# A fused attention and two-layer gated MLP on one core: explicit periods for the weight conversions and x operands among the heads, tiles laid out by their time of death, and the last heads' normalization moved to the MLP's list

## Chip, core and metric

One NeuronCore of a Trainium2 chip runs the whole program as one launch. The time is the device time of one execution in microseconds (us), as the median of several; lower is better. The engines are TensorE (PE in the rows; its weight loads are PEld), VectorE (DVE), ScalarE (ACT), GpSimd (POOL) and SyncE (SP, which here only issues transfers; SPq and ACTq are the rows of queues).

## What is computed

Causal attention with a position bias over 4 batches of 8 heads, 576 positions, head size 64; its output, as 2304 tokens of 512 features, goes through two gated layers of width 1536, both with weights that arrive as 64-bit floats:

```python
cum = np.cumsum(np.maximum(s, 0.0), axis=-1)
bias = -(cum[:, :, :, None] - cum[:, :, None, :])
scores = np.where(causal, -1e9, q @ k.T / sqrt(64) + np.minimum(bias, 0.0))
attn = softmax(scores) @ v
x = attn.transpose(0, 2, 1, 3).reshape(2304, 512)
x = (sigmoid(x @ w_gate) * (x @ w_val)) @ w_out
out = ((x @ w_a) * (x @ w_b)) @ w_out2
```

## The kernel before, in words

**Two lists.** The program is two functions, `attention` and `mlps`, each of which fills a `Schedule` with operations (engine, duration, closure, dependencies, priority, a pool slot that it takes or gives back) and emits them. Every engine then runs its own instructions strictly in the emitted order, and waits at the first one whose inputs or buffers are not ready. `attention` is emitted with `in_order=True`: always the ready operation with the lowest priority number, where an operation whose pool has no free slot is passed over until one is given back. The priorities are places on a nominal time line in periods of HT = 6.1 us, one per head; head i begins at 6.1 i. `mlps` is emitted by the list's own simulation: each engine takes the lowest-numbered operation that is ready at the simulated time, with the durations and latencies (`lat`) that the operations carry.

**The heads.** Per head PE computes row maxima's scores (L550, L555), transposes the maxima (L570), computes the transposed scores (L587, L588) and the product with v (L624). ACT splits q and k (L520, L521), copies the transposed maxima out of PSUM (L572, "mc") and sends them on (L574), takes the exponentials (L593) and copies the product (L633, "xc"). The maxima's PSUM tile `ps_t` is used again by the last piece of the transposed scores, so PE's L587 on `ps_t` waits for ACT's L572. DVE takes maxima (L563) and low parts (L524, L526); POOL masks (L609) and normalizes (L637, "xm"). The normalization of a pair of heads is a chain through memory: L635 stores the sums, L651 and L652 invert them, L660 stores, L657 spreads them over the partitions ("rb"), L637 multiplies, L641 stores the pair into `x_sb` ("xd"). SP issues nearly all transfers, one queue for all of them, the small ones `o<-rel` (L530) and `o<-relq_d` (L531) of each head among them.

**Weights among the heads.** A matrix half (512 KB of 64-bit words) is loaded into one of three `raw` tiles (L194, "wl"), turned to 32 bits by one ACT instruction (L215) and four DVE instructions (L216 to L223), and gate and value halves are combined (`combine`): sums on DVE (L255, "ws"), high parts on ACT (L265, "wh"), low parts on POOL (L268, "wr"). The third piece of `wr` in order gives back the first `raw` tile of a pair, the last gives back the second. Six halves are converted among the heads (three column blocks of the first layer's weights), two of the three pairs are also combined there. Before, half e was placed at period 4e-2, with ACT's first step 2 periods later and `combine` spread over the 14 periods after the second half; with three `raw` tiles, halves 3, 4 and 5 find no free tile at their own priority.

**x operands.** The MLP multiplies by Strassen-like seven products, each in high and low parts (three matmuls, `passes`, L289 to L291). For each of three token blocks the operands are four sums (L317, "xs"), seven high parts on ACT (L320, "xh"), and seven low parts (L323, "xl"). Those of block 0 are made among the last heads (sums on POOL, low parts on DVE); the sums lie in two `stg` tiles.

**The MLP.** For each layer 12 column blocks c of the weights times 3 token blocks b give 36 units of 42 matmuls; a unit's results go through ACT (L780), DVE (L783, L794) and POOL (L796) to memory (`hd`, L798). The down product then reads them back (L859), splits them (L862 on ACT, L863 on DVE) and multiplies. Its input slots lie in one of the three operand regions (`H0`, `H1` in that of block 1), and the later half of its weights (L842, L843) in that of block 0; both need that block's last unit to be done (`last_of`).

**Memory.** `alone` opens one pool per tile. Attention's tiles grow from the right end of SBUF, the constants and the MLP's tiles from the left. A tile of the MLP that covers an address of attention waits for the last use of what lay there. Before, the order of declaration was not chosen: `wk2`, `rg1`, `rg2`, then `s0` to `s7` and `hs0` to `hs2` from the left; `rb`, `xt`, `xp`, `sc` at the right end, so that `s` and `hs` lie where `rb`, `xt` and `xp` lay.

Of the kernel before, what the change touches and what calls it, by code (L numbers as in the profile page):

```python
# [119 lines left out]
def attn_mlp_kernel(  # L120
# [14 lines left out]
    nc = tc.nc  # L135
# [112 lines left out]
    def combine(sc, n, done, prio, at):  # L248
# [22 lines left out]
        sc.op(("ws", n, 0), "DVE", 0.85, lambda: sums(0), list(done), prio + at[0], acq=("W", n))  # L271
        sc.op(("ws", n, 1), "DVE", 0.85, lambda: sums(1), [("ws", n, 0)], prio + at[1])
# [55 lines left out]

    def attention():
        with ExitStack() as c2:  # L330
# [6 lines left out]
            pdr = c2.enter_context(tc.tile_pool(name="at_dr", bufs=1, space=bass.MemoryType.DRAM))  # L337
# [7 lines left out]
            NO, NR2, NX = 4, 3, 5  # L345
            small = tile1([128, 1], FP32, "small")
            base = small[:, 0:1]
            rb_t = [tile1([128, S], FP32, f"rb{i}") for i in range(2)]
            xt = [tile1([128, S], FP32, f"xt{i}") for i in range(NX)]
            xp = [tile1([128, S], FP32, f"xp{i}") for i in range(2)]  # L350
            sc_t = [tile1([128, S // D], FP32, f"sc{i}") for i in range(2)]

            vx_t = [tile1([128, NC, 2 * D], FP32, f"vx{i}") for i in range(2)]

            P0 = [0, 576, 1024, 1344, 1536]
# [3 lines left out]
            mkb = tile1([128, 256], BF16, "mkb")  # L359
            mr_t = [tile1([NC, 128], F32R, f"mr{i}") for i in range(3)]  # L360
            nm_t = [tile1([128, 8], FP32, f"nm{i}") for i in range(4)]

            CQ1, CK1 = 0, 640
            o_t = [tile1([128, CK1 + S], F32R, f"o{i}") for i in range(NO)]
            p_t = [tile1([128, 2 * S], F32R, f"o2_{i}") for i in range(3)]
            r_t = [tile1([128, S], FP32, f"r{i}") for i in range(NR2)]
# [4 lines left out]
            rel = tile1([128, 2, S], F32R, "rel")  # L373
            sel, neg1 = pt_t[1][0:NR, S:2 * S], pt_t[2][0:3, S:2 * S]
            stg = [tile1([128, 2 * NP], FP32, f"stg{i}") for i in range(2)]
# [286 lines left out]

            for i in range(NH):
                head(i)

            for e in range(6):
                n, m = e // 2, e % 2
                prio = HT * (4 * e - 2) + WLATE * (e == 0)
                last = convert(sc, n, m, [("S", 4 * e - 3, 0)], prio,
                               at=[2 * HT + 1.2, 3 * HT - 0.15, 3 * HT - 0.14, 4 * HT - 0.15, 5 * HT - 0.15])  # L670
                if m == 1 and n < 2:
                    combine(sc, n, [prev_last, last], prio,
                            [6 * HT - 0.15, 10 * HT - 0.15] + [(7 + j) * HT + 0.2 if j == 0 or j == 3 else (10 + j) * HT + 0.2 for j in range(4)]
                            + [(11 + j) * HT + 3.2 for j in range(4)])
                prev_last = last
# [3 lines left out]
            done = [("xd", i) for i in range(H)]  # L679
            for k, (name, p, q, _) in enumerate(XS):  # L680
                op(("xs", name), "Pool", 2.1, x_sum(nc.gpsimd, get, 0, k), done + [("xs", z) for z in (p, q) if z[0] == "S"] + [("xs", "S3")] * (name == "S4"),
                   HT * (23 + k + (k > 1)) + 3.5, acq=("stg", name))
            for k, name in enumerate(["S3", "S1", "A11", "S2", "A12", "A22", "S4"]):
                op(("xh", name), "ACT", 0.75, x_high(rg, get, 0, name), done + [("xs", name)] * (name[0] == "S"), HT * (24 + k) + 1.7)
                op(("xl", name), "DVE", 0.96, x_low(nc.vector, rg, get, 0, name), [("xh", name)] + [("xs", z) for z in BEFORE[name]], HT * (25 + k) - 0.15,
# [4 lines left out]
    def mlps():  # L690
        def tile1(shape, dtype, name):
            return alone(ctx, shape, dtype, name)

        wslot.append(tile1([128, 2, WC], F32R, "wk2"))
# [280 lines left out]
```

## Time and profile before

| | us |
|---|---|
| median of 3 runs (lowest, highest) | 1125.54 (1125.07, 1128.4) |
| the profiled execution | 1125.24 |
| its span, first to last instruction | 1123.5 |
| PE busy in the span | 1049.9 (93%) |
| DVE, ACT, POOL busy | 723.9, 476.8, 384.2 |
| mean granted TensorE clock | 0.971 |

The heads fill about the first 254 us of the span, the first layer's units and down product the time to about 693 us, the second layer the rest. A row of a timeline has the start, the duration (of a merged row the length it covers), the engine, the line, the operation, what is written and read, and in square brackets how long the engine stood idle before it and what ended that. A row of waits has the total, the count and the longest. A row of windows has, per engine, busy time and the number of instructions begun, then the granted TensorE clock, where 1.00 is the 2.4 GHz level and 0.50 the 1.2 GHz level.

### The profile page before, as it was taken

The numbers are of one execution on the slowest core, as the hardware profiler recorded it, in microseconds if no ns is written. First come the engines' busy times: TensorE is split into PE (matmuls) and PEld (weight loads), VectorE is DVE, ScalarE is ACT, GpSimd is POOL, SyncE is SP. The second block draws the span as 40 slices with busy tenths as digits, with TensorE's granted clock in tenths as the row PEclk, the third lists the DMA queues.
The fourth block names the chain that finished last, engine by engine and source line by source line (L and its number), as shares of the span: only waits on it lengthen the run. The fifth ranks groups of instructions, "written<-read, shape, count | busy, mean of one in ns | idle before, by whom it ended". The sixth has DMA issues, their size and how long they took to land.

```text
span 1123.5 us, 16123 instructions
## 1 busy us (share of the span) xinstructions
PE 1049.9 (93%) x5638; PEld 955.7 (85%) x5638; DVE 723.9 (64%) x1137; ACT 476.8 (42%) x890; POOL 384.2 (34%) x363
## 2 busy tenths in 40 slices
PE   6999597894899999999899999899999999899998
PEld 4878486683899999999788889799999999788886
DVE  6786576765947876566983626966886676942222
ACT  3665364554445544455543325423443333422221
POOL 4135245556424452343320203525543333300000
PEclk9999898896999999999999999999999999899999
DMA  5466465443114433233664333214423224643342
GB/s 146 130 174 173 118 166 149 124 113 120 43 46 132 128 117 110 94 123 141 230 192 133 115 95 127 66 57 131 132 94 132 75 100 160 201 138 114 114 122 94
DMA packets 105871, 139.55 MB, mean 124 GB/s; under 512 B 32547, under 2 KB 67035, under 8 KB 105790
## 3 DMA queue, kind: packets, MB, share of 16 engines
q1 hardware_dynamic: 102542, 133.57, 38.2%
q10 hardware_dynamic: 2896, 4.81, 1.7%
q8 instruction: 44, 0.72, 0.2%
q14 instruction: 37, 0.30, 0.1%
q0 software_dynamic: 352, 0.16, 0.1%
HBM read 85.43 MB, written 33.33 MB: 106 GB/s over the span
## 4 chain that ended last, share of the span: by engine, by line
PE 78%; DVE 7%; DMA 5%; issue 4%; POOL 3%; ACT 1%; SPq 1%; ACTq 0%; POOLq 0%; DVEq 0%
PE ps L291 22%; PE ps L289 22%; PE ps L290 22%; PE ps_x L624 5%; PE ps_g L550 2%; POOL xp L637 1%; DVE hs L317 1%; PE ps_e L587 1%; PE ps_e L588 1%; PE ps_g L555 1%; DVE s L783 1%; POOL wk L268 1%; DVE nm L563 1%; DVE u L218 1%; DMA raw<-in_moe_w_val_dram 1%
## 5 line engine op out<-in xcount | busy, mean ns | idle before, releaser
L289 PE MATMUL ps<-rg,wk 128*128 128x384 f32 (+2 forms) x1128 | 385.3, 342 | 27.3 <-ACT s L780 19.3
L291 PE MATMUL ps<-rg,wk 128*128 128x384 f32 (+2 forms) x1128 | 383.7, 340 | 0.0
L289 PEld LDWEIGHTS ps<-rg,wk 128*128 128x128 f32 x1128 | 213.9, 190 | 35.3 <-ACT s L780 21.9
L291 PEld LDWEIGHTS ps<-rg,wk 128*128 128x128 f32 x1128 | 213.9, 190 | 3.8
L783 DVE TENSOR_TENSOR s<-ps,s 128x384 f32<-128x384 f32 x216 | 118.3, 553 | 125.6 <-PE ps L291 72.4
L290 PE MATMUL ps<-x_sb,wk 128*128 128x384 f32 x576 | 193.6, 336 | 0.0
L290 PE MATMUL ps<-rg,wk 128*128 128x384 f32 (+2 forms) x552 | 190.2, 345 | 2.1 <-DVE rg L863 2.1
L780 ACT COPY s<-ps 128x384 f32<-128x384 f32 x216 | 103.1, 480 | 185.5 <-PE ps L291 184.4
L796 POOL TENSOR_TENSOR hs<-s,s 128x384 f32<-128x384 f32 x72 | 80.4, 1116 | 264.5 <-issue 94.1
L268 POOL TENSOR_TENSOR wk<-raw,wk 128x512 fp32r<-128x512 f32 (+1 forms) x96 | 129.1, 1370 | 94.6 <-PE ps L291 54.8
L863 DVE TENSOR_TENSOR rg<-rg 128x512 fp32r<-128x512 f32 (+1 forms) x120 | 82.9, 699 | 116.3 <-ACT rg L862 114.3
L862 ACT CAST rg<-rg 128x512 fp32r<-128x512 f32 (+1 forms) x120 | 68.2, 577 | 159.3 <-DMA rg<-hd 128.6
L290 PEld LDWEIGHTS ps<-rg,wk 128*128 128x128 f32 x552 | 105.0, 190 | 6.2 <-DVE rg L863 2.4
L624 PE MATMUL ps_x<-pt,vx 128*128 128x256 f32 (+1 forms) x434 | 105.9, 387 | 4.2 <-ACT xt L633 2.9
L290 PEld LDWEIGHTS ps<-x_sb,wk 128*128 128x128 f32 x576 | 108.9, 189 | 0.3
L563 DVE TENSOR_REDUCE nm<-ps_g 128x1 f32<-128x512 f32 (+4 forms) x154 | 74.5, 534 | 41.2 <-PE ps_g L555 40.8
L624 PEld LDWEIGHTS ps_x<-pt,vx 128*128 128x128 f32 x434 | 80.1, 201 | 23.2 <-ACT xt L633 3.8
L609 POOL TENSOR_SCALAR_AFFINE_SELECT pt<-pt 128x256 f32<-128x256 f32 (+1 forms) x96 | 43.1, 468 | 132.9 <-ACT pt L593 132.0
L289 PE MATMUL ps<-rg,rg 128*128 128x512 f32 (+1 forms) x228 | 86.1, 378 | 0.0
L290 PE MATMUL ps<-rg,rg 128*128 128x512 f32 (+1 forms) x228 | 86.1, 378 | 0.0
L291 PE MATMUL ps<-rg,rg 128*128 128x512 f32 (+1 forms) x228 | 86.1, 378 | 0.0
L215 ACT ACTIVATE mag<-raw 128x512 f32<-128x512 f32 x72 | 48.5, 673 | 66.9 <-DVE raw L223 36.0
(110 smaller groups left out, 1549.8 us busy)
## 6 DMA issues: line engine op xcount, KB each, us to landing
hd<-hs SPq DMA_DIRECT2D x72, 384.0 KB
rg<-hd SPq DMA_DIRECT2D x72, 256.0 KB
raw<-in_moe_w_out_dram SPq DMA_DIRECT2D x24, 512.0 KB
r<-in_qk_dram SPq DMA_DIRECT2D x32, 288.0 KB
rg<-hd SPq DMA_DIRECT2D x72, 128.0 KB
raw<-in_moe_w_gate_dram SPq DMA_DIRECT2D x12, 512.0 KB
raw<-in_moe_w_val_dram SPq DMA_DIRECT2D x12, 512.0 KB
raw<-in_moe_w_a_dram SPq DMA_DIRECT2D x12, 512.0 KB
```

What stands on the lines that cost most here:

```text
L215: ("ACT", 0.6, lambda: nc.scalar.activation(out=mag, in_=parts(n, m)[1].bitcast(FP32), func=ACTF.Abs)),
L268: return lambda: nc.gpsimd.tensor_tensor(out=wcols(n, a, w, 1), in0=src(), in1=f32(wcols(n, a, w, 0)), op=ALU.subtract)
L289: nc.tensor.matmul(out=outp, lhsT=wh, rhs=xh, start=start and e == 0, stop=False, skip_group_check=True)
L290: nc.tensor.matmul(out=outp, lhsT=wh, rhs=xl, start=False, stop=False, skip_group_check=True)
L291: nc.tensor.matmul(out=outp, lhsT=wl, rhs=xh, start=False, stop=stop and e == n - 1, skip_group_check=True)
L563: nc.vector.tensor_reduce(out=nm[0:n, c:c + 1], in_=ps[0:n, p0:p0 + nk], axis=AX.X, op=ALU.max)
L624: nc.tensor.matmul(out=px[:, 256 + a:256 + q1_], lhsT=vx[:, j], rhs=pt[:, p0:p0 + q1_ - a], start=j == 0, stop=j == js[-1])
L780: op((x,) + key, "ACT", ACT_P, lambda x=x: nc.scalar.copy(out=s(x), in_=bank("X")), [P(p)], end(p) - 2, acq=("s", key + (x,)))
L783: return lambda: nc.vector.tensor_tensor(out=s(x), in0=bank(b_), in1=s(x), op=ALU.add)
L796: op(("h2",) + key, "Pool", PTT, lambda: nc.gpsimd.tensor_tensor(out=half(1), in0=s("s4"), in1=s("s2"), op=ALU.mult), [("c22",) + key, (g[ ...
L862: op(("hh",) + key, "ACT", 0.17 + 0.00083 * N, lambda hs=hs, N=N: nc.scalar.copy(out=hs()[:, 0, 0:N], in_=f32(hs()[:, 1, 0:N])), [("hl",) ...
L863: op(("ho",) + key, "DVE", 0.157 + 0.00104 * N, lambda hs=hs, N=N: nc.vector.tensor_tensor(out=hs()[:, 1, 0:N], in0=f32(hs()[:, 1, 0:N]), ...
```

## The change

The weight halves get explicit periods: a load, ACT's first step and DVE's steps for each of the six, and `combine` of the two pairs in 4 successive periods right after its sums. The x operands of block 0 get their own periods for sums, high parts and low parts. Attention's tiles are declared by their time of death: those of the last normalizations (`xt`, `rb`, `xp`, `sc`) in a stack of their own, `tails`, at the right end, then the others, the first to die on the inner side; on the MLP's side `s` and `hs` come first, then `rg1` and `wk2`, and `rg2` only when block 2 first asks for it, when `tails` is closed. Ten operations of the last four heads (the spread of pair 14, the whole chain of pair 15 after its sums, the four products, the two stores) are taken out of attention's list and put at the head of the MLP's. The simulation's latencies of weight sums, operand sums and high parts in the MLP rise from 0.2 to 1.0, 1.2 and 0.6 us. The last column block's units run in the order 1, 0, 2 of the token blocks instead of 0, 1, 2.

```diff
@@ convert / combine @@
-        sc.op(("ws", n, 0), "DVE", 0.85, lambda: sums(0), list(done), prio + at[0], acq=("W", n))
-        sc.op(("ws", n, 1), "DVE", 0.85, lambda: sums(1), [("ws", n, 0)], prio + at[1])
+        sc.op(("ws", n, 0), "DVE", 0.85, lambda: sums(0), list(done), prio + at[0], acq=("W", n), lat=1.0)
+        sc.op(("ws", n, 1), "DVE", 0.85, lambda: sums(1), [("ws", n, 0)], prio + at[1], lat=1.0)
@@ attention @@
+            def tile2(shape, dtype, name):
+                return alone(tails, shape, dtype, name, side="right")
...
+            xt = [tile2([128, S], FP32, f"xt{i}") for i in range(NX)]
+            rb_t = [tile2([128, S], FP32, f"rb{i}") for i in range(2)]
+            xp = [tile2([128, S], FP32, f"xp{i}") for i in range(2)]
+            sc_t = [tile2([128, S // D], FP32, f"sc{i}") for i in range(2)]
...
+            LATE = NH // 2 - 2
             for i in range(NH):
                 head(i)
-
-            for e in range(6):
+            for n in [("rb", LATE)] + [(k, j) for k in ("rc", "rd", "rb") for j in range(LATE + 1, NH // 2)] + \
+                    [("xm", i) for i in range(2 * LATE, NH)] + [("xd", j) for j in range(LATE, NH // 2)]:
+                late[n] = sc.ops.pop(n)
+
+            LOADS = [(-1, 1, 2), (2, 4, 5), (5, 8, 10), (12, 13, 14), (13, 16, 19), (20, 21, 22)]
+            SUMS = [(8, 9, 9), (17, 18, 17)]
+            for e, (ld, ab, dv) in enumerate(LOADS):
                 n, m = e // 2, e % 2
-                prio = HT * (4 * e - 2) + WLATE * (e == 0)
-                last = convert(sc, n, m, [("S", 4 * e - 3, 0)], prio,
-                               at=[2 * HT + 1.2, 3 * HT - 0.15, 3 * HT - 0.14, 4 * HT - 0.15, 5 * HT - 0.15])
+                prio = HT * ld + (0.5 if e > 2 else 0)
+                last = convert(sc, n, m, [("S", max(ld - 1, 0), 0)], prio,
+                               at=[HT * ab + 1.2 - prio] + [HT * (dv + k) - 0.15 + y - prio for k, y in ((0, 0), (0, 0.01), (1, 0), (2, 0))])
                 if m == 1 and n < 2:
-                    combine(sc, n, [prev_last, last], prio,
-                            [6 * HT - 0.15, 10 * HT - 0.15] + [(7 + j) * HT + 0.2 if j == 0 or j == 3 else (10 + j) * HT + 0.2 for j in range(4)]
-                            + [(11 + j) * HT + 3.2 for j in range(4)])
+                    s0, s1, h0 = SUMS[n]
+                    combine(sc, n, [prev_last, last], 0.0,
+                            [HT * s0 - 0.15, HT * s1 - 0.15] + [HT * (h0 + k) + 0.2 for k in (0, 2, 1, 3)] + [HT * (h0 + k) + 3.2 for k in (0, 2, 1, 3)])
...
+            AT_S = {"S1": 23, "S3": 24, "S2": 26, "S4": 28}
+            AT_H = {"A11": 24, "S3": 25, "S1": 26, "S2": 27, "A22": 28, "S4": 29, "A12": 30}
+            AT_L = {"S3": 26, "S1": 28, "A11": 29, "S2": 30, "A22": 30.2, "A12": 31, "S4": 31.2}
-                   HT * (23 + k + (k > 1)) + 3.5, acq=("stg", name))
-            for k, name in enumerate(["S3", "S1", "A11", "S2", "A12", "A22", "S4"]):
+                   HT * AT_S[name] + 3.5, acq=("stg", name))
...
@@ mlps @@
+        s_t = [tile1([128, NP], FP32, f"s{i}") for i in range(8)]
+        hs_t = [tile1([128, 2 * NP], FP32, f"hs{i}") for i in range(3)]
+        region.append(tile1([128, RC], F32R, "rg1"))
         wslot.append(tile1([128, 2, WC], F32R, "wk2"))
-        region.extend(tile1([128, RC], F32R, f"rg{i}") for i in (1, 2))
...
+            if k == len(region):
+                tails.close()
+                region.append(tile1([128, RC], F32R, f"rg{k}"))
...
-        op("tail", "Pool", 4.0, lambda: None, [], -1000)
+        op("tail", "ACT", 1.0, lambda: None, [], -1000)
+        op("sd", "SP", 0.5, lambda: None, ["tail"], -999, lat=2.5)
+        for k, (nm, (eng, dur, fn, deps, _, _, _, _)) in enumerate(late.items()):
+            op(nm, eng, dur, fn, deps + ["tail" if nm == ("rb", 14) else "sd"], -500 + k, lat={"rd": 3.5, "rb": 3.5, "xd": 3.0}.get(nm[0]))
...
-            return [(c, b) for b in range(NBK) for c in range(3)] + [(c, b) for c in range(3, KF) for b in range(NBK)]
+            return [(c, b) for b in range(NBK) for c in range(3)] + [(c, b) for c in range(3, KF - 1) for b in range(NBK)] + [(KF - 1, b) for b in (1, 0, 2)]
...
+            if L == 0 and b == 2:
+                deps = [k for k in late if k[0] == "xd"]
```

## Rows read from the trace of the kernel before

**Rows 1.** Waits of PE, 0 to 300 us: total us, times, longest
```profile
PE ps_t L587 <- ACT mr L572: 19.9, 4, 5.7
PE ps L289 <- ACT s L780: 15.7, 2, 13.9
```
**Rows 2.** Waits of PE, 296 us to the end (all of them)
```profile
PE ps L289 <- DVE s L783: 5.0, 2, 3.3
PE ps L289 <- ACT rg L862: 4.4, 2, 2.3
PE ps L289 <- ACT s L780: 3.6, 4, 1.3
PE ps L290 <- DVE rg L863: 2.1, 1, 2.1
PE ps L291 <- DVE rg L863: 1.3, 1, 1.3
```
**Rows 3.** Timeline of ACT, the first and last of four stops
```profile
116.46 0.68 ACT L215 ACTIVATE mag<-raw 128x512 f32<-128x512 f32 x1 [7.75 <-DMA raw<-in_moe_w_val_dram]
...
200.78 0.83 ACT L320 CAST rg<-stg 128x768 fp32r<-128x768 f32 x1 [6.31 <-POOL stg L317]
```
**Rows 4.** Timelines of POOL and SP, what those two stops waited behind
```profile
111.07 1.29 POOL L268 TENSOR_TENSOR wk<-raw,wk 128x512 fp32r<-128x512 f32 x1
...
112.80 0.40 SPq L194 DMA_DIRECT2D raw<-in_moe_w_val_dram  x1
...
198.44 2.31 POOL L317 TENSOR_TENSOR stg<-x_sb 128x768 f32<-128x768 f32 x1
```
**Rows 5.** Timeline of ACT, L572 of heads 14, 18, 22, 26 and 31
```profile
103.35 0.26 ACT L572 CAST mr<-ps_t 5x128 fp32r<-5x128 f32 x1 [0.61 <-PE ps_t L570]
...
144.94 0.26 ACT L572 CAST mr<-ps_t 5x128 fp32r<-5x128 f32 x1 [2.52 <-PE ps_t L570]
...
169.19 0.26 ACT L572 CAST mr<-ps_t 5x128 fp32r<-5x128 f32 x1 [0.49 <-PE ps_t L570]
...
209.48 0.26 ACT L572 CAST mr<-ps_t 5x128 fp32r<-5x128 f32 x1 [2.69 <-PE ps_t L570]
...
241.67 0.26 ACT L572 CAST mr<-ps_t 5x128 fp32r<-5x128 f32 x1 [1.94 <-PE ps_t L570]
```
**Rows 6.** Timelines of SP and PE, a weight load among undisturbed heads
```profile
58.52 0.60 SPq L194 DMA_DIRECT2D raw<-in_moe_w_gate_dram  x1
...
66.30 0.70 PE L550 MATMUL ps_g<-o 128*128 128x512 f32 x3 [1.05 <-DMA o<-relq_d]
```
**Rows 7.** Timelines of POOL, DVE, ACT and PE where the MLP begins
```profile
263.52 2.86 POOL L637 TENSOR_TENSOR xp<-xt,rb 64x576 f32<-64x576 f32 x2 [1.87 <-DMA rb<-rr_d]
...
272.81 5.05 POOL L323 TENSOR_TENSOR rg<-hs,rg 128x768 fp32r<-128x768 f32 x2
...
266.42 0.96 DVE L317 TENSOR_TENSOR hs<-x_sb 128x768 f32<-128x768 f32 x1 [8.96 <-POOL xp L637]
...
269.61 2.08 DVE L317 TENSOR_TENSOR hs<-x_sb 128x768 f32<-128x768 f32 x1
...
267.41 0.83 ACT L320 CAST rg<-hs 128x768 fp32r<-128x768 f32 x1 [10.54 <-DVE hs L317]
...
270.81 0.69 PE L289 MATMUL ps<-rg,wk 128*128 128x384 f32 x1 [13.85 <-ACT s L780]
...
276.64 0.34 PE L291 MATMUL ps<-rg,wk 128*128 128x384 f32 x1
...
278.75 0.34 PE L291 MATMUL ps<-rg,wk 128*128 128x384 f32 x1
```
**Rows 8.** Windows of 5 us where the two down products begin, and a steady one
```profile
540.00:545.00 5.00, 2.87 (x8) 2.20 (x8) 5.00 (x8) 4.03 (x8) 2.50 (x2) 0.78 1.01 387
...
555.00:560.00 5.00, 5.00 (x24) 4.14 (x23) 4.83 (x7) 2.84 (x5) 1.68 (x1) 1.00 0.68 221
...
965.00:970.00 5.00, 3.54 (x9) 2.73 (x10) 5.00 (x9) 3.21 (x7) 0.98 (x1) 0.60 0.94 321
```

More of the change, by code (lines that the diff above doesn't have):

```diff
@@ L326, in attn_mlp_kernel @@
     BEFORE = {"A11": ["S2", "S3"], "A12": ["S4"], "A22": ["S1"], "S1": ["S2"], "S2": ["S4"], "S3": [], "S4": []}
+    late = {}
+    tails = ExitStack()
     def attention():
@@ L335, in psum1 @@
                 return alone(c2, [128, n], FP32, name, space=PSUM)
[L337 removed]
+            def tile2(shape, dtype, name):
+                return alone(tails, shape, dtype, name, side="right")
+            pdr = tails.enter_context(tc.tile_pool(name="at_dr", bufs=1, space=bass.MemoryType.DRAM))
             SUP = 1.0 / scale
@@ L359, in attention @@
             mkb = tile1([128, 256], BF16, "mkb")
+            nm_t = [tile1([128, 8], FP32, f"nm{i}") for i in range(4)]
+            stg = [tile1([128, 2 * NP], FP32, f"stg{i}") for i in range(2)]
             mr_t = [tile1([NC, 128], F32R, f"mr{i}") for i in range(3)]
-            nm_t = [tile1([128, 8], FP32, f"nm{i}") for i in range(4)]
-            CQ1, CK1 = 0, 640
             o_t = [tile1([128, CK1 + S], F32R, f"o{i}") for i in range(NO)]
             p_t = [tile1([128, 2 * S], F32R, f"o2_{i}") for i in range(3)]
+            rel = tile1([128, 2, S], F32R, "rel")
             r_t = [tile1([128, S], FP32, f"r{i}") for i in range(NR2)]
@@ L372, in attention @@
             mkf, zer = pt_t[1][:, 0:128], pt_t[2][:, 0:S]
-            rel = tile1([128, 2, S], F32R, "rel")
             sel, neg1 = pt_t[1][0:NR, S:2 * S], pt_t[2][0:3, S:2 * S]
-            stg = [tile1([128, 2 * NP], FP32, f"stg{i}") for i in range(2)]
             def load_qk(i):
@@ L699, in rgn @@
         def rgn(L, b):
-            return region[(b + 2 * L) % NBK]
+            k = (b + 2 * L) % NBK
+            if k == len(region):
+                tails.close()
+                region.append(tile1([128, RC], F32R, f"rg{k}"))
+            return region[k]
         NH_ = RC // (2 * NB)
         sc = Schedule({
-            "s": [tile1([128, NP], FP32, f"s{i}") for i in range(8)],
-            "hst": [tile1([128, 2 * NP], FP32, f"hs{i}") for i in range(3)],
+            "s": list(s_t),
+            "hst": list(hs_t),
             "ps": [alone(ctx, [128, 512], FP32, f"ps{i}", space=PSUM) for i in range(8)],
@@ L709, in mlps @@
             "W": [wslot[2]],
-            "H0": [rgn(0, 1)[:, i * 2 * NB:(i + 1) * 2 * NB].rearrange("p (e t) -> p e t", e=2) for i in range(NH_)],
-            "H1": [rgn(1, 1)[:, i * 2 * NB:(i + 1) * 2 * NB].rearrange("p (e t) -> p e t", e=2) for i in range(NH_)],
+            "H0": [region[1][:, i * 2 * NB:(i + 1) * 2 * NB].rearrange("p (e t) -> p e t", e=2) for i in range(NH_)],
+            "H1": [region[0][:, i * 2 * NB:(i + 1) * 2 * NB].rearrange("p (e t) -> p e t", e=2) for i in range(NH_)],
         })
@@ L815, in operands @@
                 op(("xs", L, b, name), "DVE", 0.96, x_sum(nc.vector, get, b, k),
-                   deps + [("xs", L, b, z) for z in (p, q) if z[0] == "S"] + [("xs", L, b, "S3")] * (name == "S4"), t0 + k, acq=("hst", (L, b, name)))
+                   deps + [("xs", L, b, z) for z in (p, q) if z[0] == "S"] + [("xs", L, b, "S3")] * (name == "S4"), t0 + k, acq=("hst", (L, b, name)), lat=1.2)
             for k, name in enumerate(["S3", "S1", "A11", "S2", "A12", "S4", "A22"]):
-                op(("xh", L, b, name), "ACT", 0.81, x_high(rg, get, b, name), deps + [("xs", L, b, name)] * (name[0] == "S"), t0 + 2 + k)
+                op(("xh", L, b, name), "ACT", 0.81, x_high(rg, get, b, name), deps + [("xs", L, b, name)] * (name[0] == "S"), t0 + 2 + k, lat=0.6)
                 eng = ("DVE", "Pool")[k % 2]
```

14 lines of the change are left out of this document (6 added, 8 removed).

## The prediction

> **What bounds the kernel now.** The page first: PE is busy 93% of the span, so what can be gained without removing matmuls is its idle time and the time at the lower clock. The waits of PE say where the idle time sits. Up to 300 us it has two large entries: 19.9 us in four stops on ACT's L572, and 15.7 us on L780 with one stop of 13.9 us [rows 1]. Behind 296 us there are only ten stops, 16.4 us together [rows 2]. None of these entries names the converted weights `wk` as what PE waited for. So the change must be read at four places: the heads, the start of the MLP, the periods in which x operands are made, and the starts of the two down products.
>
> **The heads.** ACT shows what lies under the four stops [rows 3]. In three of them (the first is shown) it stands 7.6 to 7.8 us at L215, the first step of a weight conversion, until the load lands; in the last it stands 6.3 us at a high part until POOL has made the sum. ACT works in order, so L572 stands behind. The cause is the order: the load was emitted only when `wr` gave a `raw` tile back, and the conversion's first step, long due, right behind it. POOL's `wr` ends at 112.36, SP issues at 112.80, ACT starts at 116.46 [rows 3, 4]: nothing covers these 4 us. Likewise POOL ends the sum at 200.75 and ACT starts at 200.78.
>
> What the stops cost is more than PE's wait, since the work after them runs late and at the lower clock. The starts of L572 give it [rows 5]. Heads 18 to 22, without a stop, take 24.25 us, a pace of 6.06. Heads 14 to 18 take 41.59, 17.3 more; heads 22 to 26 take 40.29, 16.0 more. Sum 33.4 us.
>
> After the change halves 3, 4 and 5 are due at periods 12, 13 and 20, and `combine` gives the tiles back at 11, 12 and 19 (plus 3.2 us), so each load is emitted at its own place. ACT's first step comes 1, 3 and 1 periods later; the sums of POOL stand 4.3 nominal us ahead of their high parts. All four stops should go: **-33.4**.
>
> What is late next: a load among undisturbed heads. Half 2 at 58.52 delayed `o<-relq_d`, issued behind it on SP, and PE stood 1.05 us at 66.30 [rows 6]. Halves 3, 4 and 5, until now hidden in the stops, will each do that, and for 3 and 5 ACT's step follows one period (6.1 nominal) plus 0.7 after the load's place, while the load alone takes 3.66 from issue to use [rows 3, 4] and SP runs behind its nominal place by an amount that no row here gives. I bound each by 0 and 3 us (most of an uncovered load) and take 1.5, 0.7 (half 4, three periods ahead) and 1.5, near the 1.05 that was seen: +3.7. Half 2 moves one period ahead, away from the spread of `rb` in the same queue: -1.0, bounds 0 and -1.05. The fifteen steps of halves 3 to 5 on ACT and DVE and the moved pieces of `combine` run one or two per period in the gaps that PE's 6.06 us leave the other engines; I cost them at nothing. Without that cover each would cost its 0.7 (L215) to 1.3 us (L268) [rows 3, 4].
>
> Heads 26 to 31 take 32.19, 1.9 above the pace [rows 5]; there DVE made one low part of x in nearly every period. Now only three of seven lie in periods with full head work. I take half: -1.0, bounds 0 and -1.9. **Heads together: -31.7**, from -24 to -36.
>
> **The start of the MLP.** PE does its first two products and stops for 13.85 us until 270.81 [rows 7]. The chain back: ACT's L780 stands behind a high part that waits for DVE's sum into `hs`; that waits 8.96 us for POOL's last products `xp` (263.52 to 266.38), because `hs` lies over their tiles. After the stop, 18 matmuls take 5.83 us (270.81 to 276.64), where the 12 behind them take 2.11, so 0.176 each: 2.7 us at the lower clock. Together with the other stops on L780, 15.7-13.85 = 1.85 [rows 1], 18.4 us.
>
> The new layout puts `s` and `hs` over `r`, `rel` and `o2`, dead before the last product with v, `rg1` and `wk2` over tiles dead when it ends. What still waits for `xp` is `rg2`, which unit (0, block 2) needs six units later: 6 x 42 x 0.176 = 44 us, while the chain now ends 9.4 us after PE's stop began (266.38 against 256.96). Moved with it to the MLP's list: on DVE two instructions; on POOL four products, 5.7 us; on SP seven transfers, ahead of which stands a weight load that nothing needs for nine units (66 us), and behind which stand the first stores of `hd`; these hold three `hst` tiles, one of which a unit takes every 7.4 us. DVE's L651 in this chain waits for its sums, with the first `c11` addition queued behind; POOL's products wait for `rb`, with the first L796 behind. PE reaches those only after some 2 and 8 us, about when they come free.
>
> Now POOL is the full one. In the three units before block 1 is due (22.2 us) it has four products (5.7), four `wr` at 1.3 (5.2) [rows 4], three low parts at 2.5 (7.6) and two L796 (about 2.2, an estimate from half the width): 20.7. That fits, barely; I leave 1.5 us of stops. **-16.9**, from -9 to -18.4.
>
> Here a rule speaks against the change. In the rows a sum on DVE takes 0.96 us, and the same 2.08 while POOL works on `wk` [rows 7]. The Trainium skill (SBUF — State Buffer, Who interferes with whom) says that a DVE instruction with two SBUF inputs and a GpSimd instruction that reads SBUF exclude each other for their whole length. The trace agrees with the direction; what full exclusion would make of this stage is the first rival.
>
> **x operands in the MLP.** L783 and L780 stop PE for 8.6 us after 296 [rows 2], where DVE is behind with sums and low parts of the next blocks and ACT waits in order for them. The raised latencies place ACT's high parts later and so its copies for PE earlier, and without the arrears of the start DVE is less behind. The same reordering can also misplace something: bounds +2 and -7, taken **-3.5**, a little under the middle of what is there.
>
> **The down products.** PE stops 4.4+2.1+1.3 = 7.8 us for L862 and L863 [rows 2]. Around them the clock is 0.78 and 0.60 [rows 8]: at the 5.00/24 = 0.208 us per matmul of the steady window, 2.87 and 3.54 us of busy time hold 13.8 and 17, but 8 and 9 were done: 5.8 and 8 too few, 2.9 us. Of 10.7, the new order of the last units frees the input slots one unit, 7.4 us, earlier, three times the longest stop. The price is that the later weights' region comes free a unit later; they are needed only from the seventh of twelve steps on, 6 x 4 x 3 x 0.208 = 15 us into the product. ACT and DVE remain full of conversions, so **-9**, from -4 to -10.7.
>
> **Sum.** -31.7-16.9-3.5-9.0 = -61.1. The rows are of an execution of 1125.24 (span 1123.5 and 1.7 around it), 0.3 below the median of 1125.54, so both give **1064**. All good ends give 1053, all bad ends 1090.
>
> **Rivals.**
>
> *POOL and DVE exclude each other.* Then POOL's 20.7 and DVE's eight sums and low parts at 0.96 (7.7) add to 28.4 against 22.2: 6.2 us more stop at block 1, and the operand periods gain nothing (3.5): 1074. For it: 2.08 against 0.96. Against: POOL's 2.5 already holds some of the waiting, and DVE is idle before the MLP begins. This follows the rule named above.
>
> *The loads come too late among the heads.* Halves 3 to 5 cost 3 us each, half 2 and DVE's low parts give nothing: heads -24, 1072. For it: 3.66 us alone, and 1.05 us seen from a load not even waited for. Against: three halves were loaded among heads without a stop on L215.
>
> *The layout does not do what it says:* if `s` or `hs` still touched the late tiles, the start would gain nothing, 1081. The sizes speak against it: `s` and `hs` need 21.5 KB per partition, `r`, `rel` and `o2` hold 25.3.
>
> *Slower:* the weight sums' latency of 1.0 pushes the conversions of the 21 column blocks made in the MLP behind other work, and PE waits for `wk` at the first product of each block. It decides from 61.1/21 = 2.9 us per block. Against: no wait of PE on `wk` anywhere now, and conversions are listed 24 us ahead.
>
> **How the numbers follow.** The forecast gets 0.60, the first rival 0.18, the second 0.12, the layout 0.05, no net change 0.02, slower 0.03. A change of 0.3%, 3.4 us, is about what a measurement of this kernel can tell from none. Every case but the last two is faster by more: 0.95, 0.02, 0.03. The range goes from nearly all good ends, 1054, to the first two rivals together (1081) with a little of the down products' bad end, 1085.
>
> **What would show it.** Right: PE's waits up to 300 us without the four stops on L572, ACT's idle time before L215 under 3 us in all, heads 14 to 26 in about 77 us instead of 106, PE past its first products without the 13.85, `hs` waiting for no `xp`, L862 and L863 gone from PE's waits. Wrong: L215 or L320 again ahead of L572, PE waiting for low parts from POOL (L323) at block 1, or a new entry on `wk`.

## Result and the profile after

The changed kernel takes 1076.16 us (median of 4, 1074.29 to 1077.49); the kernel before, on the same chip, 1126.42 (1125.07 to 1128.4). The ratio is 0.9551 [0.9529, 0.9574]: 50.3 us faster, where 61 were predicted; 1076.16 lies in the predicted range. The profiled execution took 1075.38, with a span of 1073.4 and a mean granted clock of 0.992, before 0.971. In the changed kernel the lines of `attention` from L380 on stand one lower (L530 and L531 are L529 and L530, L572 is L571, L587 is L586), and in the MLP 17 to 19 higher (L780 is L797, L783 is L800, L862 is L881).

From the page of the changed kernel, the engines' busy times:

```profile
PE 1035.8 (96%) x5638; PEld 945.8 (88%) x5638; DVE 716.4 (67%) x1137; ACT 474.7 (44%) x890; POOL 390.2 (36%) x363
```

Where the time came from, by five places of the timeline (us). Each place is the start of a first product, so a stop ahead of the first down product is counted with the units:

| | before | after | gain |
|---|---|---|---|
| start to the first product of the MLP | 254.59 | 232.64 | 21.95 |
| first layer's units | 285.16 | 267.86 | 17.3 |
| first down product | 154.11 | 152.00 | 2.1 |
| second layer's units | 271.34 | 267.58 | 3.8 |
| second down product | 153.05 | 148.84 | 4.2 |

Waits of PE in the changed kernel, 0 to 300 us (total, times, longest), the two largest; they answer to [rows 1]:

```profile
PE ps_g L549 <- DMA o<-relq_d: 6.9, 3, 3.0
PE ps L289 <- ACT s L797: 4.5, 4, 2.0
```

The 19.9 us on L572 are gone, and of the 15.7 on L780 4.5 are left. In their place stands a wait that was small before: PE's first score product of a head on the transfer `o<-relq_d`, three stops, one for each of the halves 3, 4 and 5.

Waits of PE from 235 us to the end, the two largest; they answer to [rows 2]:

```profile
PE ps L289 <- DVE s L800: 7.4, 4, 3.0
PE ps L289 <- ACT s L797: 4.5, 4, 2.0
```

The waits on L862 and L863 are gone. None on `wk` has come.

Timeline of ACT in the changed kernel: L571 of heads 14, 23, 26 and 31, which answer to [rows 5], and the first step of halves 3, 4 and 5, which answers to [rows 3]:

```profile
105.03 0.66 ACT L215 ACTIVATE mag<-raw 128x512 f32<-128x512 f32 x1 [2.55 <-DMA raw<-in_moe_w_val_dram]
105.61 0.24 ACT L571 CAST mr<-ps_t 5x128 fp32r<-5x128 f32 x1
...
124.67 0.68 ACT L215 ACTIVATE mag<-raw 128x512 f32<-128x512 f32 x1
...
159.88 0.66 ACT L215 ACTIVATE mag<-raw 128x512 f32<-128x512 f32 x1 [3.38 <-DMA raw<-in_moe_w_val_dram]
...
168.51 0.26 ACT L571 CAST mr<-ps_t 5x128 fp32r<-5x128 f32 x1 [2.32 <-PE ps_t L569]
...
187.22 0.26 ACT L571 CAST mr<-ps_t 5x128 fp32r<-5x128 f32 x1 [0.83 <-PE ps_t L569]
...
218.38 0.26 ACT L571 CAST mr<-ps_t 5x128 fp32r<-5x128 f32 x1 [1.94 <-PE ps_t L569]
```

Heads 14 to 26 take 187.22-105.61 = 81.6 us, before 106.1. ACT still waits for the load in halves 3 and 5, but 2.55 and 3.38 us instead of over 7; half 4 waits for nothing. Timeline of SP around half 4, and of PE at the three stops:

```profile
107.83 0.54 SPq L194 DMA_DIRECT2D raw<-in_moe_w_gate_dram  x1
108.58 0.61 SPq L529 DMA_DIRECT2D o<-rel  x1
109.24 0.62 SPq L530 DMA_DIRECT2D o<-relq_d  x1
```

```profile
105.27 0.71 PE L549 MATMUL ps_g<-o 128*128 128x512 f32 x3 [1.63 <-DMA o<-relq_d]
...
113.76 0.73 PE L549 MATMUL ps_g<-o 128*128 128x512 f32 x3 [2.24 <-DMA o<-relq_d]
...
160.65 0.77 PE L549 MATMUL ps_g<-o 128*128 128x512 f32 x3 [2.99 <-DMA o<-relq_d]
```

The load of 512 KB is issued 0.75 us ahead of the next head's two small transfers, and PE stands until the second of them lands. Half 4 shows it best: ACT's first step on it comes 17 us after the load, and still PE lost 2.24 us. Half 2 in the same kernel shows when such a load costs nothing (timelines of SP and PE):

```profile
53.00 0.42 SPq L194 DMA_DIRECT2D raw<-in_moe_w_gate_dram  x1
...
54.95 0.28 SPq L530 DMA_DIRECT2D o<-relq_d  x1
...
60.17 0.71 PE L549 MATMUL ps_g<-o 128*128 128x512 f32 x3
```

There `relq_d` stands 1.95 us behind the load, but PE needs it only 5.2 us after it was issued. For halves 3, 4 and 5 `relq_d` was issued at 100.94, 109.24 and 155.96, and without its stop PE would have needed it 2.7, 2.3 and 1.7 us later; it came 4.3 to 4.7 us after its issue.

Timeline of PE and POOL in the changed kernel where the MLP begins; they answer to [rows 7]:

```profile
232.64 0.44 PE L289 MATMUL ps<-rg,wk 128*128 128x384 f32 x1 [1.20 <-ACT xt L632]
235.37 0.45 PE L289 MATMUL ps<-rg,wk 128*128 128x384 f32 x1 [0.38 <-ACT s L797]
...
251.35 0.44 PE L289 MATMUL ps<-rg,wk 128*128 128x384 f32 x1 [1.99 <-ACT s L797]
```

```profile
230.44 3.05 POOL L636 TENSOR_TENSOR xp<-xt,rb 64x576 f32<-64x576 f32 x2 [1.27 <-DMA rb<-rr_d]
...
234.75 6.29 POOL L268 TENSOR_TENSOR wk<-raw,wk 128x512 fp32r<-128x512 f32 x4 [1.27 <-issue]
241.00 4.26 POOL L636 TENSOR_TENSOR xp<-xt,rb 64x576 f32<-64x576 f32 x2
...
247.75 3.42 POOL L636 TENSOR_TENSOR xp<-xt,rb 64x576 f32<-64x576 f32 x2
```

The stop of 13.85 us is 0.38 now, though the last products `xp` are not done until 251.17. With this one there are five stops on L797 and L800 up to 300 us, 5.3 us in all (4.5 and 0.8); the one at 251.35 is the longest.

### The profile page after: what moved, and what is told of

Read it like the earlier page. It is cut to its first block, busy times and chain, and to the rows that moved or that the text cites. A ratio compares the mean times of both kernels' runs of the same rounds, so it can differ in the third digit from the quotient of the medians.

```text
span 1073.4 us, 16121 instructions
## 1 busy us (share of the span) xinstructions
PE 1035.8 (96%) x5638; PEld 945.8 (88%) x5638; DVE 716.4 (67%) x1137; ACT 474.7 (44%) x890; POOL 390.2 (36%) x363
## 4 chain that ended last, share of the span: by engine, by line
PE 80%; DVE 7%; issue 4%; DMA 4%; POOL 3%; ACT 2%; SPq 1%; ACTq 0%; POOLq 0%; DVEq 0%
PE ps L289 24%; PE ps L290 24%; PE ps L291 24%; PE ps_x L623 4%; POOL xp L636 2%; PE ps_g L549 1%; POOL pt L608 1%; DVE x_sb L323 1%; PE ps_e L586 1%; PE ps_e L587 1%; DMA o<-relq_d 1%; DVE s L800 1%; PE ps_g L554 1%; DVE hs L317 1%; DVE u L216 1%
## 5 line engine op out<-in xcount | busy, mean ns | idle before, releaser
L800 DVE TENSOR_TENSOR s<-ps,s 128x384 f32<-128x384 f32 x216 | 118.7, 552 | 128.6 <-PE ps L291 73.3
L797 ACT COPY s<-ps 128x384 f32<-128x384 f32 x216 | 103.2, 480 | 180.6 <-PE ps L291 179.7
L268 POOL TENSOR_TENSOR wk<-raw,wk 128x512 fp32r<-128x512 f32 x96 | 125.4, 1336 | 98.0 <-ACT wk L265 87.7
L882 DVE TENSOR_TENSOR rg<-rg 128x512 fp32r<-128x512 f32 (+1 forms) x120 | 85.5, 721 | 112.3 <-ACT rg L881 106.3
L881 ACT CAST rg<-rg 128x512 fp32r<-128x512 f32 (+1 forms) x120 | 68.2, 578 | 149.1 <-DMA rg<-hd 112.9
L623 PE MATMUL ps_x<-pt,vx 128*128 128x256 f32 (+1 forms) x434 | 99.7, 370 | 2.5 <-ACT xt L632 1.6
L623 PEld LDWEIGHTS ps_x<-pt,vx 128*128 128x128 f32 x434 | 76.0, 191 | 19.9 <-ACT xt L632 2.6
L215 ACT ACTIVATE mag<-raw 128x512 f32<-128x512 f32 x72 | 48.4, 672 | 70.9 <-DVE raw L223 43.0
```

Source lines behind the costliest of these rows:

```text
L268: return lambda: nc.gpsimd.tensor_tensor(out=wcols(n, a, w, 1), in0=src(), in1=f32(wcols(n, a, w, 0)), op=ALU.subtract)
L623: nc.tensor.matmul(out=px[:, 256 + a:256 + q1_], lhsT=vx[:, j], rhs=pt[:, p0:p0 + q1_ - a], start=j == 0, stop=j == js[-1])
L797: op((x,) + key, "ACT", ACT_P, lambda x=x: nc.scalar.copy(out=s(x), in_=bank("X")), [P(p)], end(p) - 2, acq=("s", key + (x,)))
L800: return lambda: nc.vector.tensor_tensor(out=s(x), in0=bank(b_), in1=s(x), op=ALU.add)
L881: op(("hh",) + key, "ACT", 0.17 + 0.00083 * N, lambda hs=hs, N=N: nc.scalar.copy(out=hs()[:, 0, 0:N], in_=f32(hs()[:, 1, 0:N])), [("hl",) ...
L882: op(("ho",) + key, "DVE", 0.157 + 0.00104 * N, lambda hs=hs, N=N: nc.vector.tensor_tensor(out=hs()[:, 1, 0:N], in0=f32(hs()[:, 1, 0:N]), ...
```

## The experiments

Times are medians of four executions, ratios against the kernel before on the same chip: 1125.11 for x1 to x4, 1126.57 for x5 to x8, 1124.83 for x9 to x12. In x4, x9 and x10 the lines behind L183 stand one higher than in the changed kernel.

**Which wait costs the heads their 10 us?** Three theories. The queue (A): the small transfers stand behind the load on SP. The step (B): ACT's L215 comes too early, and what stands behind it on ACT is late. Bandwidth (C): 512 KB takes the DMA engines from everything, wherever it is issued. The first run moves the steps of halves 3 and 5 one period later, the second the loads 1.6 us later, behind the head's small transfers, the third both, and the fourth leaves places as they are and issues the same loads from ACT.

```diff
@@ x1 @@
-            LOADS = [..., (12, 13, 14), (13, 16, 19), (20, 21, 22)]
+            LOADS = [..., (12, 14, 15), (13, 17, 19), (20, 22, 23)]
@@ x2 @@
-                prio = HT * ld + (0.5 if e > 2 else 0)
+                prio = HT * ld + (2.1 if e > 2 else 0)
@@ x4 @@
+        eng = nc.scalar if (n, m) in ((1, 1), (2, 0), (2, 1)) else nc.sync
-            nc.sync.dma_start(
+            eng.dma_start(
```

> The conversion steps of halves 3 and 5 (ACT's first one and DVE's four) one period later, loads where they are. In the changed kernel heads 13 to 23 take 71.1 us (L571 at 97.42 and 168.51) against 60.2 at the pace of 6.02; PE stops 6.9 us on o<-relq_d and ACT 5.9 us ahead of L215 in halves 3 and 5. Theory A (the two small transfers of a head stand behind the 512 KB load in SP's queue): ACT's 5.9 us go, PE's 6.9 stay, heads 13 to 23 still 70 us or more, the whole within 1.5 us of 1073.4 span. Theory B (ACT's step, due one period behind the load, holds the heads): heads 13 to 23 fall to about 64, only half 4's 2.5 us stay, span about 1066. Theory C (the memory traffic of that period is simply too much, whatever the order): within 1.5 us of the changed kernel in all four of these runs.

> The three loads 1.6 nominal us later, which puts each behind the two small transfers of its period in SP's queue and changes nothing else. Theory A: PE's 6.9 us on o<-relq_d go; ACT now waits longer ahead of L215 for halves 3 and 5 (its 5.9 us grow to about 9), which PE feels on L571; half 4, three periods ahead of its step, costs nothing: heads 13 to 23 about 66 us, span about 1068. Theory B: longer than the changed kernel, heads 13 to 23 about 74. Theory C: no change.

> Both edits: loads behind the small transfers, steps of halves 3 and 5 one period later. Theory A: both waits gone, heads 13 to 23 about 62 us (the pieces of combine keep about 1), span about 1064, about 9 us under the changed kernel. Theory B: as with the later steps alone, about 64. Theory C: no change. If this is the fastest of the four it is the candidate for a better version.

> The three loads issued from ACT at the same place of the list instead of from SP, so the small transfers no longer stand behind them in one queue, while the memory traffic and its time stay. Theory A: PE's stops on o<-relq_d fall from 6.9 to under 2 us; the wait ahead of L215 stays or shrinks (ACT's queue reaches the load earlier than SP's), heads 13 to 23 about 63 to 67. Theory C, contention of the 16 DMA engines whatever the queue: the stops stay at 5 us or more, heads 13 to 23 70 us or more. Rival in itself: ACT stands at the load until POOL has given the raw tile back, then L571 stands behind it and the heads are longer than 71.

| | us | ratio | starts of L571, heads 13 to 23 |
|---|---|---|---|
| before | | | 85.9 |
| changed kernel | 1076.16 | 0.9551 [0.9529, 0.9574] | 71.1 |
| x1, steps later | 1077.04 | 0.9583 [0.9548, 0.9618] | 66.1 |
| x2, loads later | 1073.98 | 0.9552 [0.9531, 0.9572] | 66.8 |
| x3, both | 1073.2 | 0.9553 [0.9515, 0.959] | 71.1 |
| x4, ACT's queue | 1070.03 | 0.9508 [0.9486, 0.953] | 65.0 |

The last column is of one execution each. The seven profiled executions that have these heads as the changed kernel has them (its own, x5 to x8, x11, x12) lie between 70.4 and 73.7.

Steps later: ACT's wait on L215 is gone, `relq_d` still has 4.0 us, and the median is no lower, though the profiled execution (1073.84) took 5 us less in these heads. Loads later: the `relq_d` wait is gone, and the next ones in line have grown. PE's waits of x2, 85 to 230 us:

```profile
PE ps_x L623 <- ACT xt L632: 4.1, 7, 1.1
PE ps_x L623 <- DMA vx<-in_vm_dram: 2.2, 3, 1.5
```

In x3 the tile `vx`, loaded behind the weights on SP, took the place: 7.7 us in five stops in its profiled execution, which with 1081.37 us was its slowest (the others took 1071.66 to 1073.34). None of the three can be told from the changed kernel by its ratio. Theory A had asked for 70 us or more in these heads for x1, and for 9 us in all from x3, and neither came. Why the shorter heads of x1 and x2 do not show in the medians stays open. In x4 `relq_d` shrinks from 6.9 us to one stop, in PE's waits, 85 to 230 us:

```profile
PE ps_g L550 <- DMA o<-relq_d: 0.5, 1, 0.5
```

Timeline of ACT in x4, the load of half 3 and its first step, at the place where the changed kernel waited 2.55 us:

```profile
93.66 0.84 ACTq L195 DMA_DIRECT2D raw<-in_moe_w_val_dram  x1
...
101.27 0.68 ACT L216 ACTIVATE mag<-raw 128x512 f32<-128x512 f32 x1
```

The edit of x4 is the queue alone, and it took the stops away. On ACT the load does not stand ahead of the head's transfers, nor, as the second row shows, behind SP's other work, so the step has no wait either. But the edit changes two things at once. ACT reaches the three loads earlier: `relq_d` is issued 4.2, 4.9 and 6.4 us behind them, where SP issued it 1.4, 1.4 and 2.0 us behind, and a load took 3.66 us from issue to use [rows 3, 4]. By this estimate the loads were over when `relq_d` went out. Whether a queue of its own or the longer lead spared the small transfers was not separated, and bandwidth is not excluded: a transfer that SP issued 0.13 us behind the load of half 4 still stopped PE. Timelines of ACT, SP and PE in x4:

```profile
100.54 0.44 ACTq L195 DMA_DIRECT2D raw<-in_moe_w_gate_dram  x1
...
100.67 0.38 SPq L382 DMA_DIRECT2D vx<-in_vm_dram  x1
...
105.53 0.89 PE L624 MATMUL ps_x<-pt,vx 128*128 128x256 f32 x4 [1.24 <-DMA vx<-in_vm_dram]
```

The Trainium skill (DMA: Bandwidth & Descriptors, Queues, rings and completion order) says that SP and ACT each own a ring on each of the same 16 DMA engines, and that an engine takes turns between rings packet by packet. The stops, 6.9 us by one ring and 0.5 by two, do not contradict it, but with the different leads no run here shows the turns.

Is the step then worth anything? x9 has both edits; beside it the changed kernel was run again:

> The three loads from ACT's queue, and the conversion steps of halves 3 and 5 one period later. With the loads on ACT's queue alone heads 13 to 23 took 65.0 us (71.1 in the changed kernel), with 1.4 and 1.1 us left in the periods of halves 3 and 5. Theory A (what costs is what stands behind the load on SP): little is left to win, heads 13 to 23 between 63 and 65, span within 2 us of that run's 1065. Theory B (ACT's step, due one period behind the load, is a cost of its own): those two periods fall to the pace, heads 13 to 23 about 62.5, span 2 to 3 us lower.

> The changed kernel once more beside the others, so that they are compared on one chip: 1074 to 1078 us, heads 13 to 23 at 71 us if the two waits belong to the order of the transfers and not to one execution.

x9, with ACT's queue and the later steps, takes 1070.5 (0.9513 [0.9499, 0.9527]) and the changed kernel 1078.08 (0.9579 [0.9555, 0.9603]): 7.6 us, and the intervals stand apart. The changed kernel lies just above the time put on record for it, and its heads 13 to 23 take 73.7 us, not 71; its three stops on `o<-rel` and `o<-relq_d` are 5.9 us. Heads 13 to 23 take 65.2 in x9 and 65.0 in x4, and the ratios agree: the steps' place adds nothing that could be measured once the loads are on ACT.

**What is each part worth?** One run has the parts for the heads alone, put into the kernel before; three undo one part each in the changed kernel.

```diff
@@ x5: column blocks in one order to the end @@
-  + [(c, b) for c in range(3, KF - 1) for b in range(NBK)] + [(KF - 1, b) for b in (1, 0, 2)]
+  + [(c, b) for c in range(3, KF) for b in range(NBK)]
@@ x6: the latencies of ws, xs and xh back to the default @@
-  ..., prio + at[0], acq=("W", n), lat=1.0)
+  ..., prio + at[0], acq=("W", n))
@@ x8: the ten last operations stay in attention's list @@
-            for n in [("rb", LATE)] + ...:
-                late[n] = sc.ops.pop(n)
@@ x11: before, with LOADS, SUMS and AT_S, AT_H, AT_L of the change @@
...
```

> The kernel before with the heads' part of the change alone (periods of loads, steps, combine and x operands); layout, list, latencies and unit order as before. In the changed kernel the MLP's first product came 21.95 us earlier (232.64 against 254.59). Theory: the heads' part stands by itself, first product at 231 to 234, the MLP behind it unchanged, span 1100 to 1104. Rival: part of it is taken back at the start of the MLP, where the chain of the last products decides and not PE; then the span gains less than 18.

> The changed kernel with the last column block's units back in the order 0, 1, 2 of the token blocks. In the changed kernel PE has no stop on L862 or L863 where the down products begin; from the landmarks of the two traces I put 12.7 us of the gain there. Theory: the stops come back, 7 to 8 us of idle time and 3 to 4 us at the lower clock, span 1084 to 1087. Rival: the stops went because the rest of the change gave ACT and DVE room; then the span moves by less than 3 us.

> The changed kernel with the simulated latencies of weight sums, operand sums and high parts back at 0.2. Theory: they give almost nothing; the stretch from the first layer's down product to the second's gained only 0.3 us beyond the stops of the down products; span within 2 us of 1073.4, PE's stops on the copies and additions of the units (11.9 us behind 235 us) about the same. Rival (the prediction): they place ACT's high parts behind its copies and are worth 3.5 us; the span rises by 3 to 7.

> The changed kernel with the ten operations of the last heads left at the end of attention's list; the layout and everything else stays. Theory L (the layout alone gave the start): PE runs past its first products as now, the stops from the first product of the MLP to 300 us stay at about 5 us, span within 3 us of 1073.4. Rival M (the place in the list matters): POOL is busy with the four late products until about 11 us after the MLP begins, the converted weights of the third column block and the first unit's product come behind them, PE stops 8 to 15 us more, span 1081 to 1089.

| part | run | us | ratio | worth |
|---|---|---|---|---|
| heads alone | x11 | 1101.83 | 0.9796 [0.9772, 0.982] | 1124.83-1101.83 = 23.0 |
| order of the last units undone | x5 | 1089.16 | 0.9663 [0.963, 0.9696] | 1089.16-1076.16 = 13.0 |
| move undone | x8 | 1086.67 | 0.9648 [0.9607, 0.969] | 10.5 |
| latencies undone | x6 | 1079.54 | 0.9578 [0.9549, 0.9606] | 3.4 |

Together 49.9 of the 50.3. (The runs that undo a part are set against the changed kernel's 1076.16; the kernel before took 1126.57 beside them and 1126.42 beside it.) Each of these differences is good to some 3 or 4 us (the executions of x8 lie between 1080.95 and 1091.96), so that they add up this closely is in part luck. By the medians x6 cannot be told from the changed kernel at all: 0.9578, against 0.9551 and, in x12, 0.9579. The new layout by itself has nothing left that could be measured; that it is what makes the move possible is argued from the addresses, since no run has the move with the old layout.

PE where the MLP begins, first in x11 (its L633 and L785 are the changed kernel's L632 and L797), then in x8 (its L793 is L797):

```profile
232.97 0.44 PE L289 MATMUL ps<-rg,wk 128*128 128x384 f32 x1 [0.80 <-ACT xt L633]
...
248.80 0.69 PE L289 MATMUL ps<-rg,wk 128*128 128x384 f32 x1 [13.47 <-ACT s L785]
```

```profile
241.87 0.69 PE L289 MATMUL ps<-rg,wk 128*128 128x384 f32 x1 [3.93 <-ACT s L793]
...
261.38 0.69 PE L289 MATMUL ps<-rg,wk 128*128 128x384 f32 x1 [6.36 <-ACT s L793]
```

x11 reaches the MLP when the changed kernel does (232.97 against 232.64) and keeps the long stop, so the two gains are separate. In x8, with the layout but without the move, two stops of 3.93 and 6.36 us stand in its place, and 9.5 us of the first layer's gain are lost. POOL tells why, in x8:

```profile
241.04 3.77 POOL L636 TENSOR_TENSOR xp<-xt,rb 64x576 f32<-64x576 f32 x2 [1.62 <-DMA rb<-rr_d]
244.89 6.60 POOL L268 TENSOR_TENSOR wk<-raw,wk 128x512 fp32r<-128x512 f32 x4
```

All the products `xp` come ahead of the low parts of `wk`, which in the changed kernel begin at 234.75, ahead of the last four products. Its first low parts of `rg` follow at 251.44, where the changed kernel has one at 245.34 and the next at 251.25.

PE in x5 at the starts of the two down products, whose stops in the changed kernel are gone:

```profile
500.50 0.50 PE L289 MATMUL ps<-rg,wk 128*128 128x512 f32 x1 [2.52 <-ACT rg L881]
502.25 0.79 PE L290 MATMUL ps<-rg,wk 128*128 128x512 f32 x1 [1.25 <-DVE rg L882]
...
924.80 0.79 PE L289 MATMUL ps<-wk,rg 128*128 128x512 f32 x1 [2.25 <-ACT rg L881]
926.79 0.80 PE L291 MATMUL ps<-wk,rg 128*128 128x512 f32 x1 [0.77 <-DVE rg L882]
```

They hold 6.8 us. By the places of the timeline the down products take 2.3 and 3.7 us longer than in the changed kernel, and the units ahead of them 2.65 and 2.4; the latter are the stops of 2.52 and 2.25 ahead of the first products. Around the stops the clock is low. Windows of PE and the other engines at the second down product, first in x5, then in the changed kernel (the granted clock is the third number from the end):

```profile
925.00:930.00 5.00, 4.23 (x11) 3.12 (x12) 5.00 (x8) 4.01 (x8) 1.32 (x2) 0.50 0.98 354
```

```profile
925.00:930.00 5.00, 5.00 (x24) 4.10 (x23) 5.00 (x8) 1.75 (x3) 2.14 (x3) 1.00 0.64 180
```

For x6 the text put on record ahead of it expected almost nothing. Its first layer's units take 271.47 us, where the seven profiled executions with the changed kernel's MLP (its own, x1 to x4, x9, x12) take 267.6 to 267.9: 3.6 us. Its second layer's units, 268.82, lie among the 267.6 to 271.9 of those seven. PE's waits of x6, 225 to 300 us, the two largest:

```profile
PE ps L289 <- ACT s L797: 4.5, 3, 1.7
PE ps L289 <- DVE s L800: 3.8, 1, 3.8
```

The changed kernel has the same 4.5 us on ACT there, but 0.8 on DVE.

**Do POOL and DVE hold each other up?** All low parts of the MLP's x operands go to DVE, where three of each block's seven were POOL's. If the engines only add, DVE gets fifteen more instructions (nine of them in the second layer) and PE waits longer; if they exclude each other, DVE loses nothing.

```diff
-                eng = ("DVE", "Pool")[k % 2]
+                eng = "DVE"
```

> All seven low parts of an operand block in the MLP on DVE, none on POOL. The changed kernel stops PE 11.9 us behind 235 us on copies and additions (4.5 and 7.4), in the periods in which operands are made and DVE and POOL are both full. Theory E (DVE and POOL hold each other up): eleven instructions on DVE alone at 0.96 (10.6 us) are less than eight at about 2.1 beside POOL (16.8); the stops fall under 6 us, span about 1068. Rival (DVE is simply the full engine there): three more instructions a block make the stops longer by 3 to 8 us, span 1077 to 1081.

x7 takes 1069.28 (0.95 [0.9468, 0.9532]), 6.9 us less. PE's stops behind 235 us fall from 11.9 to 8.1, not under the 6 that was put on record. Groups of DVE and POOL from 300 us on (line, operation, count, busy time, mean ns, idle time before), the low parts in the changed kernel, then in x7:

```profile
L323 DVE TENSOR_TENSOR x_sb<-x_sb,rg 128x768 fp32r<-128x768 f32 x9 | 16.5, 1854 | 0.0
...
L323 DVE TENSOR_TENSOR rg<-hs,rg 128x768 fp32r<-128x768 f32 x3 | 3.1, 1042 | 0.0
...
L323 POOL TENSOR_TENSOR rg<-hs,rg 128x768 fp32r<-128x768 f32 x6 | 14.5, 2427 | 38.3 <-ACT rg L320 38.3
L323 POOL TENSOR_TENSOR x_sb<-hs,rg 128x768 fp32r<-128x768 f32 x3 | 6.8, 2268 | 5.0 <-ACT rg L320 5.0
```

```profile
L323 DVE TENSOR_TENSOR rg<-hs,rg 128x768 fp32r<-128x768 f32 x9 | 10.0, 1126 | 0.0
L323 DVE TENSOR_TENSOR x_sb<-x_sb,rg 128x768 fp32r<-128x768 f32 x9 | 9.6, 1072 | 0.0
...
L323 DVE TENSOR_TENSOR x_sb<-hs,rg 128x768 fp32r<-128x768 f32 x3 | 2.8, 946 | 0.0
```

Of the 21 low parts of the second layer, twelve cost DVE 19.6 us beside POOL's nine (21.3 us); all 21 cost it 22.4 without them. The nine that POOL took were worth 2.8 us of DVE's time. In the whole kernel DVE's busy time is 713.5 us with the fifteen instructions more, against 716.4, and POOL's falls from 390.2 to 356.2. That is what the rule of the first rival says (the Trainium skill, SBUF — State Buffer, Who interferes with whom), and the mean of the same instruction, 1854 ns against 1072, agrees with it.

**All that helped.** ACT's queue, later steps, and all low parts on DVE:

> The loads on ACT's queue, the steps of halves 3 and 5 one period later, and all low parts of the MLP's operands on DVE: the candidate for a better version. If the gains add (8.2 us of the heads in the run with the loads on ACT's queue, 2.3 and 1.4 us of the two layers' units in the run with the low parts on DVE): span 1060 to 1063, time about 1063, 12 to 14 under the changed kernel's 1076.2. Rival: the two share a cause (DVE and POOL busy at the start of the MLP) and give no more than the better of them, 1069.

x10 takes 1064.92 (1062.89 to 1065.35), 0.9463 [0.9448, 0.9477]: the best of the study, 13.2 us under the changed kernel on the same chip, about 7.6 by the loads on ACT's queue and 5.6 by the low parts. PE's waits from 220 us on, the two largest:

```profile
PE ps L290 <- DVE s L801: 6.9, 4, 3.4
PE ps L290 <- ACT s L798: 1.6, 3, 0.6
```

The stops behind ACT's copies are 1.6 us, where the changed kernel had 4.5; those on DVE's sums into `s` are what is left.

## Why the prediction was right and wrong

| term | predicted | bounds given | measured |
|---|---|---|---|
| heads | -31.7 | -36 to -24 | -23.0 (x11) |
| start of the MLP | -16.9 | -18.4 to -9 | -10.5 (x8) |
| x operands and latencies | -3.5 | -7 to +2 | -3.4 (x6) |
| order of the last units | -9.0 | -10.7 to -4 | -13.0 (x5) |
| sum | -61.1 | | -50.3 (the terms: -49.9) |

The direction and the mechanisms came as forecast: the four stops on L572, the stop of 13.85 and the waits on L862 and L863 are gone, and no wait on `wk` came. Two of the signs that were named did not come: ACT's idle time before L215 is 5.9 us, not under 3, and heads 14 to 26 take 81.6 us, not about 77. The sizes of three terms were off.

*Heads: this step failed,* and the term lies just outside its bounds. "I bound each by 0 and 3 us (most of an uncovered load) and take 1.5, 0.7 (half 4, three periods ahead) and 1.5". Against the pace of 6.02 us, the heads next to these loads are longer by 2.17 (half 3), 2.51 (half 4) and 3.03+2.05 (half 5): 9.8 us. Half 4 shows what was wrong. It was priced low because its step comes three periods later, as if ACT's wait were the cost; the cost is in the two small transfers behind the load on SP. The row for this was there, 1.05 us at [rows 6], but a single stop was taken for the usual size. The size depends on how late SP is with `relq_d`: 5.2 us ahead of its use at half 2, where nothing stopped, 1.7 to 2.7 us ahead at halves 3 to 5. The prediction said that no row gave this lateness. Half 2's own term came: from head 8 to head 9 it is 6.02 us instead of 7.31, 1.3 less, where 1.0 was put. Of the other terms, the heads 26 to 31 take 31.16 us and gain the 1.0 given to the low parts; the heads 12, 13, 20 and 21, with pieces of `combine`, are longer by 0.48+0.17+0.52+0.5 = 1.7 us, where nothing was put. The way from head 31 to the first product is 1.3 us longer, with a stop of 1.20 on `xt`, and head 3 begins 1.15 us later. The last need be no effect of the change: over the executions profiled here head 3 begins between 34.0 and 38.0 us with the same code ahead of it.

So the second rival, loads too late among the heads (heads -24, 1072), described the heads, and half of its grounds was the right one: 1.05 us "seen from a load not even waited for".

*Start of the MLP.* The chain was right, the estimate of what stays was not. "20.7. That fits, barely; I leave 1.5 us of stops": 5.3 us stayed in five stops. That is 3.8 of the 6.4 us by which the term missed; the rest stays open. The sum counted POOL's time and left out what POOL does to DVE; the first rival had it. x7 shows its direction and not its size: with the low parts on DVE the first layer's units take 265.59 us instead of 267.86, 2.3 where the rival asked for 6.2, and 3.7 us of stops on L797 and L800 stay up to 300 us. What makes those was not tried. That the rival's 1074 lies nearer to 1076 than the forecast is chance, since the heads made the larger part of the error.

*Latencies.* Right in size, as far as 3.4 us by the medians and 3.6 in the first layer's units can tell. The reason given, ACT's copies earlier, is not shown: where x6 loses its time, PE's stops on those copies are the same 4.5 us, and the 3.0 us more are on DVE's additions. Why DVE is later there stays open.

*Order of the last units.* By the medians 13.0, above the upper end of 10.7; by the traces 11.1 (2.65+2.3+2.4+3.7), about at it, with the 2.4 uncertain, since the second layer's units vary by 4 us among executions. The mechanism was right: 6.8 us of stops in x5 for the 7.8 before, and most of the rest lies where the clock is low, 0.50 at 925 to 930 us in x5, 1.00 in the changed kernel. The term was 9 because ACT and DVE would remain full of conversions, and that reserve was not needed. The 1.9 us between medians and traces are within the noise: x5 was profiled in its fastest execution, 1083.56 us, and its slowest took 1090.81.

The errors, +8.7, +6.4, +0.1 and -4.0, add to 11.2, about the 10.8 by which the forecast missed; with terms good to some 3 or 4 us each, this closeness is luck as well.

## What to carry over

Price a transfer put into a busy in-order queue by what stands behind it there, not only by when its own data is needed: half 4 had 17 us to spare and still cost 2.5 us, while half 2 cost nothing, because what stood behind it was issued early enough. Moving the load within that queue passed the wait to the next one in line (`vx`, `xt`), while a second issuing engine, which also reached the load earlier, removed it. And an instruction given to POOL "beside" DVE is worth only what remains after both have slowed: in the second layer nine low parts of 21.3 us on POOL saved DVE 2.8 us, and giving all fifteen back made the kernel 6.9 us faster.

## What was not expected of the hardware

Three loads of 512 KB cost 6.9 us of stops when SP issued them 1.4 to 2.0 us ahead of a small transfer that PE waits for, and 0.5 us when ACT issued them, 4.2 to 6.4 us ahead of it. The bytes were the same; how much of this is the queue and how much the lead is not shown. And DVE's subtraction of 128x768 took 0.95 to 1.13 us on average where POOL had no low parts, while the largest group took 1.85 beside them, with POOL's own at 2.27 to 2.43.
